# Sparse attention with a SOLU layer on one core: masks moved from GpSimd to TensorE and VectorE, products with V in a rhythm of two, one and none, later turns of k and q by DMA

## The chip, the cores and the metric

One core of a Trainium2 chip runs the kernel. The metric is device microseconds of one execution. TensorE (PE) multiplies, ScalarE (ACT) evaluates exp and ln, VectorE (DVE) and GpSimd (POOL) work on elements, SyncE (SP) issues most DMAs. Each engine works through its own instructions in order; semaphores tie them together.

## What is computed

Block-sparse attention (4 batches, 8 heads, 768 positions, 64 columns a head), then a layer on the 3072 x 512 rows that come out of it:

```python
mask = (|blk_i - blk_j| <= 1) | first or last block | sampled blocks      # blocks of 32
attn = softmax(where(mask, q @ k.T / 8, -1e9))
x    = attn @ v                       # to rows of 512: all heads of one position
h    = x @ w_in                       # 512 -> 1024
solu = h * softmax(h)
out  = (solu - mean) / sqrt(var + 1e-6) * g_ln @ w_out                    # 1024 -> 512
```

## The kernel before

The loop runs over 144 units `s` (L610), each one score block: `where(s)` gives the pass `kp` (12 passes; a pass is 256 query positions of one batch `b`), the head pair `a` (4) and `j`, a third of the keys (3). So three units make the keys of one head pair, 12 units a pass, 36 a batch. The steps of a unit:

- `score` (L321): four matmuls of 64 rows, two heads side by side in rows 0 to 63 and 64 to 127, into one of three PSUM buffers of the pool `p_s`; then one exp of 128x1024 on ScalarE into `ex` (6 buffers).
- `mask` (L335), one unit later: `ex` times a 0/1 mask kept in `mask_sb`. From unit 12 on, the middle third (`j` = 1) goes to GpSimd, the others to VectorE.
- `outs` (L343), `LAG` = 3 units later: eight matmuls with V into the single buffer `op` of the pool `p_op`. V has a column of ones, so the sum of the softmax comes with it.
- `normalise` (L359), after the products of `j` = 2: a reciprocal and a multiplication on VectorE, from `op` into `xb`. The next head pair's first product needs `op` back.

Beside this, `later` (L540) holds work by unit number, run after the unit's own steps and in the order in which it was entered. A pass gives two tiles of 128 rows of the second layer; 22 of the 24 tiles run inside the loop, one per six units, from unit M0 = 18 on. A tile `t`: `moe_x` (DMA transpose `xT`), `moe_h` in two halves of four matmuls and an exp, where `h` lies in a buffer of `p_s` from its first half until `moe_u` has multiplied it with the exp (`solu`); `moe_t` (DMA transpose `lnT`), `moe_b` (statistics, ending in `vpe`), `moe_r` (ln and exp for 1/sqrt), `moe_o` (eight matmuls in four pairs), `moe_y` (scaling on ScalarE into `ot`, and the store). The last two tiles form the tail, with transposes on TensorE.

For the batches 1 to 3, `later` also loads k, q and v of a head pair (384 KB each), casts them on GpSimd (`cast_st`, `cast_v`), and turns k and q on TensorE (`turn_kq`: six transposes into a buffer of `p_s`, and a VectorE copy). Scaling w_out with g_ln and taking its column mean away (`scale_w`, `centre_w`) are 16 GpSimd instructions in units 10 to 19. The masks are built by `make_mask` from 24-row matmuls of `vis_t` (which block sees which) with `onehot`. SP issues the loads, stores and all DMA transposes in program order.

Of the kernel before, what the change touches and what calls it, by code (L numbers as in the profile page):

```python
# [201 lines left out]
def kernel(  # L202
# [11 lines left out]
    nc = tc.nc  # L214
# [59 lines left out]
    ex_p = pool("ex", 6)  # L274
# [38 lines left out]


# [6 lines left out]
    def score(s):  # L321
        kp, b, r, a, j = where(s)
        ps = p_s.tile([TQ, 2, 512], FP32, tag="s", name=f"s{s}")
        for n in range(2):
            i = 2 * j + n
            for par in range(2):
                lo = 64 * par
                nc.tensor.matmul(ps[:, par, n * 256 : (n + 1) * 256],  # L328
                                 kTs[b][lo : lo + 64, a, i * TQ : (i + 1) * TQ],
                                 qTs[b][lo : lo + 64, a, r * 256 : (r + 1) * 256],  # L330
                                 start=(n == 0), stop=(n == 1), skip_group_check=True)
# [3 lines left out]
    def mask(s, eng):  # L335

        kp, b, r, a, j = where(s)
        eng.tensor_tensor(  # L338
            out=exs[s], in0=exs[s],
            in1=mask_sb[:, r * NJ + j : r * NJ + j + 1, :].broadcast_to([TQ, 2, 512]),  # L340
            op=ALU.mult)
# [37 lines left out]
    def moe_h(t, half):  # L379
        if half == 0:  # L380
            hs[t] = p_s.tile([128, 2, HF], FP32, tag="s", name=f"h{t}")
        for c in range(KD):
            nc.tensor.matmul(hs[t][:, half, :], xTs[t][:, c, :],  # L383
                             w_in_sb[:, c, half * HF : (half + 1) * HF],
                             start=(c == 0), stop=(c == KD - 1))
        if half:
            es_of[t] = mo.tile([128, d_ff], BF16, tag="e", name=f"e{t}")
            nc.scalar.activation(out=es_of[t], in_=hs[t].rearrange("p a b -> p (a b)"),  # L388
                                 func=ACT.Exp, scale=1.0, accum_out=esum_all[:, t : t + 1])
# [38 lines left out]
    def moe_y(t):  # L428
        ot = mo.tile([128, d_model], FP32, tag="ot", name=f"ot{t}")
        nc.scalar.activation(out=ot, in_=o_ps.pop(t), func=ACT.Copy, scale=rstds.pop(t))  # L430
# [10 lines left out]
    def scale_w(c):  # L441
        nc.gpsimd.tensor_scalar(out=w_out_sb[:, c, :], in0=w_out_f[:, c, :],  # L442
# [9 lines left out]
    def centre_w(c):  # L452
        nc.gpsimd.tensor_sub(out=w_out_sb[:, c, :], in0=w_out_sb[:, c, :], in1=mean_sb)  # L453
# [17 lines left out]
    onehot = setup.tile([NB, NT, TQ], BF16, name="onehot")  # L471
    nc.vector.memset(onehot, 1.0)
# [10 lines left out]
    for base, cm, sgn in ((0, -BLK, 1), (BLK - 1, BLK, -1)):  # L483
        nc.gpsimd.affine_select(out=onehot, in_=onehot, compare_op=ALU.is_ge, fill=0.0,
# [13 lines left out]
    cast_st(0, 0, 0, nc.vector.tensor_copy)  # L498
    cast_st(1, 0, 0, nc.vector.tensor_copy)
    turn_kq(0, 0, 0, nc.scalar.copy)  # L500
    turn_kq(1, 0, 0, nc.scalar.copy)
# [10 lines left out]
    mask_sb = setup.tile([TQ, PPB * NJ, 512], BF16, name="mask_sb")  # L512

    def make_mask(n, copy):
        m = p_s.tile([TQ, 2, 512], FP32, tag="s", name=f"m{n}")
        hi = min(2 * n + 2, PPB * NJ)
        for u in range(2 * n, hi):
            r, j = u // NJ, u % NJ
            for i in range(2):
                nc.tensor.matmul(m[:, u % 2, i * 256 : (i + 1) * 256], vis_k[:, 2 * j + i, :],  # L520
                                 onehot[:, r * QW : (r + 1) * QW, :],
                                 start=(i == 0), stop=(i == 1), skip_group_check=True)
        copy(out=mask_sb[:, 2 * n : hi, :], in_=m[:, 0 : hi - 2 * n, :])

    make_mask(0, nc.vector.tensor_copy)
# [4 lines left out]
    cast_v(0, 0, nc.gpsimd.tensor_copy)  # L530
    for a in range(1, NPR):
        for which in range(2):
            cast_st(which, 0, a, nc.gpsimd.tensor_copy)
        cast_v(0, a, nc.gpsimd.tensor_copy)
# [13 lines left out]
    for n in range(1, (PPB * NJ + 1) // 2):  # L548
        at((0, 4, 6, 8)[n - 1], make_mask, n, nc.vector.tensor_copy)
    for c in range(KF):  # L550
        at(10 + c // 2, scale_w, c)
        at(16 + c // 2, centre_w, c)
    at(15, mean_of_w)
    for b in range(1, B):
        s0 = (b - 1) * UP * PPB + 6
        at(s0 - 1, alloc_kq, b)
        for a in range(NPR):
            for which in range(3):
                at(s0 + 6 * a + which, load_raw, which, b, a, nc.sync)
            for which in range(2):  # L560
                at(s0 + 6 * a + 4 + which, cast_st, which, b, a, nc.gpsimd.tensor_copy)
                at(s0 + 6 * a + 6 + 2 * which, turn_kq, which, b, a, nc.vector.tensor_copy)
            at(s0 + 6 * a + 6, cast_v, b, a, nc.gpsimd.tensor_copy)
    n_tail = n_tiles - QW
    for t in range(n_tail):
        s0 = M0 + 6 * t
        at(s0, moe_h, t, 0)
        at(s0 + 1, moe_h, t, 1)
        at(s0 + 2, moe_u, t)
        at(s0 + 2, moe_t, t)  # L570
        at(s0 + 3, moe_b, t, 0)
        at(s0 + 4, moe_b, t, 1)
        at(s0 + 6, moe_r, t)
        for n in range(4):
            at(s0 + 8 + n, moe_o, t, 2 * n, 2 * n + 2)
        at(s0 + 11, moe_y, t)
# [22 lines left out]
    for off, fn, args in (  # L599
        (-1, turn_x, (t0, nc.scalar.copy)), (-1, turn_x, (t1, nc.vector.tensor_copy)),  # L600
        (0, moe_h, (t0, 0)), (0, moe_h, (t0, 1)), (1, moe_u, (t0,)), (1, moe_h, (t1, 0)),
        (1, moe_h, (t1, 1)), (2, turn_u, (t0,)), (2, moe_u, (t1,)), (3, moe_b, (t0, 0)),
# [5 lines left out]

    s = -1
    while s < n_units + LAG or later:  # L610
# [3 lines left out]
        if 1 <= s <= n_units:  # L614
            mask(s - 1, nc.gpsimd if (s - 1) % NJ == 1 and s > UP else nc.vector)
        if s >= LAG and s - LAG < n_units:
            u = s - LAG
            outs(u)
            if u % NJ == NJ - 1:
                kp, b, r, a, j = where(u)  # L620
# [60 lines left out]
```

## Time and profile before

| | |
|---|---|
| median of 3 runs | 306.6 us (306.16 to 308.51) |
| the profiled execution | 304.71 us, its span 303.0 us |
| busy in the span | PE 222.9 us (74%), DVE 208.8 (69%), ACT 193.6 (64%), POOL 165.6 (55%) |
| mean granted TensorE clock | 0.926 |
| DMA | 37.40 MB, mean 123 GB/s |

The span goes from the first to the last instruction; 1.7 us lie around it. No engine is busy throughout. Busy time of matmuls is modelled and overlaps, so the pace of TensorE is read from one start to the next. A wait is named after what ended it.

### The profile page before, as it was taken

To read this page: it belongs to the slowest core of one execution; us is meant where nothing else is said; L and a number is where in the kernel's file an instruction comes from. 1 tells how busy PE (TensorE), PEld (TensorE's weight loads), DVE (VectorE), ACT (ScalarE), POOL (GpSimd) and SP (SyncE) were. 2 spreads that over 40 slices of the span, in tenths; PEclk is the share of its full clock that TensorE was granted. 3 is DMA by queue.
4 is the path that set the end of the run, shared out by engine and by line. 5 is a ranking of instruction groups with operands and counts; after the bars stand their busy time and mean duration, and the time that the engine had idled before them with its cause. 6 is when DMAs were issued, how large, how long until landed. Compare 5 with 4: busy or idle time off the path is not lost.

```text
span 303.0 us, 5943 instructions
## 1 busy us (share of the span) xinstructions
PE 222.9 (74%) x2317; PEld 105.2 (35%) x2356; DVE 208.8 (69%) x402; ACT 193.6 (64%) x271; POOL 165.6 (55%) x121
## 2 busy tenths in 40 slices
PE   1789848196877687697688668678877977886862
PEld 1355414043433243343233334333323432333330
DVE  3867805748768877975966797797658468665770
ACT  2445625249677967775787687768758676973531
POOL 4946999967353856756354775746344253533000
PEclk9999967759999999997999999999979898997977
DMA  6999160506226649344326557483234032122103
GB/s 218 390 259 400 56 223 0 141 0 107 63 60 187 147 133 273 101 126 114 71 52 211 175 133 198 155 110 82 55 87 71 19 88 69 38 69 71 35 35 111
DMA packets 54405, 37.40 MB, mean 123 GB/s; under 512 B 37476, under 2 KB 49764, under 8 KB 54372
## 3 DMA queue, kind: packets, MB, share of 16 engines
q1 hardware_dynamic: 53572, 35.54, 42.0%
q0 software_dynamic: 528, 1.05, 1.8%
q8 instruction: 19, 0.31, 0.5%
q10 hardware_dynamic: 272, 0.39, 0.4%
q14 instruction: 14, 0.11, 0.1%
HBM read 23.07 MB, written 6.29 MB: 97 GB/s over the span
## 4 chain that ended last, share of the span: by engine, by line
DVE 37%; PE 32%; POOL 11%; DMA 8%; issue 7%; ACT 2%; SPq 1%; POOLq 0%; ACTq 0%
PE h L383 15%; PE op L353 9%; DVE solu L393 8%; DVE ex L338 8%; DVE stats L403 8%; PE s L328 5%; DMA w_out_f<-in_moe_w_out_dram 5%; POOL w_out_sb L442 5%; DVE vpe L411 4%; DVE xb L367 4%; DMA raw<-in_v_dram 3%; POOL w_out_sb L453 3%; DVE recip_all L365 2%; POOL ex L338 2%; PE o L425 2%
## 5 line engine op out<-in xcount | busy, mean ns | idle before, releaser
L333 ACT ACTIVATE ex<-s 128x1024 bf16<-128x1024 f32 x144 | 144.2, 1028 | 72.0 <-PE s L328 69.1
L338 POOL TENSOR_TENSOR ex<-ex,mask_sb 128x1024 bf16<-128x1024 bf16 x44 | 96.3, 2189 | 95.1 <-ACT ex L333 95.1
L353 PE MATMUL op<-v,ex 128*128 128x65 bf16 x1152 | 65.2, 203 | 47.4 <-DVE xb L367 39.9
L353 PEld LDWEIGHTS <-ex 128*128 128x128 bf16 x1152 | 47.2, 103 | 84.9 <-DVE xb L367 50.0
L338 DVE TENSOR_TENSOR ex<-ex,mask_sb 128x1024 bf16<-128x1024 bf16 x100 | 75.0, 758 | 2.0 <-ACT ex L333 2.0
L328 PE MATMUL s<-qT,kT 64*128 64x256 bf16 x576 | 61.9, 296 | 9.6 <-ACT ex L333 7.1
L365 DVE RECIPROCAL recip_all<-op 128x4 f32<-128x4 f32 x48 | 8.5, 177 | 66.8 <-PE op L353 66.8
L383 PE MATMUL h<-w_in_sb,xT 128*128 128x512 bf16 x175 | 53.0, 416 | 1.7 <-issue 0.9
L425 PE MATMUL o<-w_out_sb,lnT 128*128 128x512 bf16 x171 | 52.1, 386 | 2.4 <-ACT ot L430 1.3
L328 PEld LDWEIGHTS <-kT 64*128 64x128 bf16 x576 | 18.1, 96 | 69.2 <-issue 67.2
L403 DVE BATCH_NORM_STATS2 stats<-solu 128x6 f32<-128x512 bf16 x48 | 32.7, 685 | 0.0
L388 ACT ACTIVATE e<-h 128x1024 bf16<-128x1024 f32 x24 | 24.6, 1024 | 11.9 <-PE h L383 10.0
L393 DVE TENSOR_TENSOR solu<-h,e 128x1024 bf16<-128x1024 f32 x24 | 29.2, 1216 | 0.3 <-ACT e L388 0.3
L300 POOL CAST st<-raw 128x768 bf16<-128x768 f32 x30 | 26.4, 881 | 1.2 <-POOL st L300 0.9
L310 PE MATMUL tp<-ident,st 128*128 128x128 bf16 x192 | 19.5, 252 | 6.7 <-DVE st L300 5.8
L411 DVE TENSOR_TENSOR vpe<-vpe,mv 128x1 f32<-128x1 f32 x24 | 23.5, 981 | 0.8
L383 PEld LDWEIGHTS <-xT 128*128 128x128 bf16 x192 | 17.6, 106 | 15.2 <-issue 4.6
L367 DVE TENSOR_TENSOR xb<-op,recip_all 128x256 bf16<-128x256 f32 x48 | 20.4, 425 | 1.7
L304 POOL CAST v<-raw 128x768 bf16<-128x768 f32 x16 | 16.5, 1029 | 6.2 <-DMA raw<-in_v_dram 6.1
L430 ACT ACTIVATE ot<-o,rstd 128x512 f32<-128x512 f32 x24 | 16.6, 696 | 1.4 <-issue 1.4
L442 POOL TENSOR_SCALAR w_out_sb<-w_out_f,g_ln_sb 128x512 bf16<-128x512 f32 x8 | 13.8, 1736 | 5.7 <-DMA w_out_f<-in_moe_w_out_dram 5.7
L310 PEld LDWEIGHTS <-st 128*128 128x128 bf16 x192 | 14.0, 113 | 7.7 <-DVE st L300 5.8
(57 smaller groups left out, 101.2 us busy)
## 6 DMA issues: line engine op xcount, KB each, us to landing
raw<-in_k_dram SPq DMA_DIRECT2D x16, 384.0 KB, 4.0
raw<-in_v_dram SPq DMA_DIRECT2D x16, 384.0 KB, 5.6
out_dram<-ot SPq DMA_DIRECT2D x24, 256.0 KB, 2.1
raw<-in_q_dram SPq DMA_DIRECT2D x15, 384.0 KB, 4.7
w_out_f<-in_moe_w_out_dram SPq DMA_DIRECT2D x2, 1024.0 KB, 14.4
w_in_sb<-in_moe_w_in_dram POOLq DMA_DIRECT2D x1, 1024.0 KB, 13.1
raw<-in_q_dram ACTq DMA_DIRECT2D x1, 384.0 KB, 3.3
xT<-xb SPq DMA_TRANSPOSE x22, 2.4
```

The lines of the kernel that those rows point to most:

```text
L310: nc.tensor.matmul(tp[:, i, :], st[:, i, :], ident, is_transpose=True, start=(i == 0), stop=(i == NT - 1))
L328: nc.tensor.matmul(ps[:, par, n * 256 : (n + 1) * 256], kTs[b][lo : lo + 64, a, i * TQ : (i + 1) * TQ], qTs[b][lo : lo + 64, a, r * 256 : ...
L333: nc.scalar.activation(out=exs[s], in_=ps, func=ACT.Exp, scale=scale)
L338: eng.tensor_tensor(out=exs[s], in0=exs[s], in1=mask_sb[:, r * NJ + j : r * NJ + j + 1, :].broadcast_to([TQ, 2, 512]), op=ALU.mult)
L353: nc.tensor.matmul(op[:, par * QW + c, :], ex[:, par, lo : lo + TQ], vbuf[b % 2][:, a, par, 2 * j + n, :], start=(j == 0 and n + par + c = ...
L367: nc.vector.tensor_tensor(out=dst, in0=op[:, :, 0:D].rearrange("p (h c) d -> p h c d", h=2), in1=recip.rearrange("p (h c) o -> p h c o", h ...
L383: nc.tensor.matmul(hs[t][:, half, :], xTs[t][:, c, :], w_in_sb[:, c, half * HF : (half + 1) * HF], start=(c == 0), stop=(c == KD - 1))
L393: nc.vector.tensor_mul(out=solus[t], in0=hs.pop(t).rearrange("p a b -> p (a b)"), in1=es_of.pop(t))
L403: nc.vector.bn_stats(out=stats_of[t][:, i, :], in_=solus[t][:, i * HF : (i + 1) * HF])
L411: nc.vector.tensor_add(out=vpe, in0=vpe, in1=mv[:, 1:2])
L425: nc.tensor.matmul(o_ps[t], lnTs[t][:, f, :], w_out_sb[:, f, :], start=(f == 0), stop=(f == KF - 1))
L442: nc.gpsimd.tensor_scalar(out=w_out_sb[:, c, :], in0=w_out_f[:, c, :], scalar1=g_ln_sb[:, c : c + 1], scalar2=None, op0=ALU.mult)
```

## The change

- GpSimd only casts. `scale_w` and `centre_w` go to VectorE, six and five units later. The masks of the middle third from unit 12 on are no longer multiplied: four more matmuls of 24 rows in `score` add `hid` (0 where seen, -1e30 where not) onto the scores before the exp. `hid` and `onehot` are made once and copied by DMA to partitions 64 to 87 as well. All other masks are on VectorE, two units after the score instead of one.
- `outs` runs two units' products when `s` leaves 1 on division by 3 (units `s`-4 and `s`-3), one when it leaves 2, none when it leaves 0; `normalise` follows four units after the last score of its group.
- For the batches 1 to 3, k and q are turned by a DMA transpose on SP (`turn_dma`); a head pair's loads follow each other by five units instead of six, starting four units later.
- `moe_h` makes both halves at once; `moe_u` and what follows come one unit later; `moe_o` runs in pieces of two, three and three; `moe_y` scales on VectorE, but for the last tile; tile 21 starts three units earlier.
- At the start vis comes before the first casts, the first qT copy goes to VectorE beside ScalarE's kT copy, the first mask copy to ScalarE, and GpSimd casts v after the next k and q. `ex` has 7 buffers.

```diff
+    def turn_dma(which, b, a):
+        st = staged.pop((which, b, a)).rearrange("p i h d -> p (i h d)")
+        nc.sync.dma_start_transpose(
+            out=(kTs, qTs)[which][b][:, a, :].rearrange("p (i x) -> p i x", i=NT), in_=st)
...
     def score(s):
...
+        for n in range(2 if added else 0):
+            for par in range(2):
+                lo = 64 * par
+                nc.tensor.matmul(ps[:, par, n * 256 : (n + 1) * 256],
+                                 hid_k[lo : lo + NB, 2 * j + n, :],
+                                 onehot[lo : lo + NB, r * QW : (r + 1) * QW, :],
+                                 start=False, stop=(n == 1), skip_group_check=True)
...
+    def adds_mask(s):
+        return s >= UP and s % NJ == 1
...
     def moe_y(t):
...
-        nc.scalar.activation(out=ot, in_=o_ps.pop(t), func=ACT.Copy, scale=rstds.pop(t))
+        if t < n_tiles - 1:
+            nc.vector.tensor_scalar(out=ot, in0=o_ps.pop(t), scalar1=rstds.pop(t), scalar2=None,
+                                    op0=ALU.mult)
...
-        nc.gpsimd.tensor_scalar(out=w_out_sb[:, c, :], in0=w_out_f[:, c, :],
+        nc.vector.tensor_scalar(out=w_out_sb[:, c, :], in0=w_out_f[:, c, :],
...
+    def make_hid():
+        nc.vector.tensor_scalar(out=hid[0:NB], in0=vis_t.rearrange("a n o -> a (n o)"),
+                                scalar1=-1.0, scalar2=1e30, op0=ALU.add, op1=ALU.mult)
+        for t in (hid, onehot):
+            nc.sync.dma_start(out=t[64 : 64 + NB], in_=t[0:NB])
...
-                at(s0 + 6 * a + 4 + which, cast_st, which, b, a, nc.gpsimd.tensor_copy)
-                at(s0 + 6 * a + 6 + 2 * which, turn_kq, which, b, a, nc.vector.tensor_copy)
+                at(s0 + 5 * a + 5 + which, cast_st, which, b, a, nc.gpsimd.tensor_copy)
+                at(s0 + 5 * a + 7 + which, turn_dma, which, b, a)
...
+        s0 = M0 + 6 * t - (3 if t == n_tail - 1 else 0)
+        at(s0, moe_h, t)
+        at(s0 + 3, moe_u, t)
...
-            mask(s - 1, nc.gpsimd if (s - 1) % NJ == 1 and s > UP else nc.vector)
-        if s >= LAG and s - LAG < n_units:
-            u = s - LAG
-            outs(u)
...
+        todo = {1: (s - 4, s - 3), 2: (s - 3,), 0: ()}[s % NJ]
+        for u in todo:
+            if 0 <= u < n_units:
+                outs(u)
...
+        if 2 <= s <= n_units + 1:
+            mask(s - 2)
```

On VectorE, from a mask of tile 5 to the normalise of the next group, before (exNN is unit NN's exp, opK_A the products of pass K and head pair A):

```order
L338 TENSOR_TENSOR ex51_1530<-ex51_1530,mask_sb_196 128x1024
L403 BN_STATS stats5_1544<-solu5_1521 128x6
L406 BN_AGGR mv5_1567<-stats5_1544 128x2
L409 TENSOR_SCALAR vpe5_1569<-esum_all_62 128x1
L411 TENSOR_TENSOR vpe5_1569<-vpe5_1569,mv5_1567 128x1
L365 RECIPROCAL recip_all_61<-op4_0_1533 128x4
L367 TENSOR_TENSOR xb4_1588<-op4_0_1533,recip_all_61 128x2x2x64
L338 TENSOR_TENSOR ex53_1577<-ex53_1577,mask_sb_196 128x1024
L312 COPY kT2_1267<-tp02_1_1615 128x768
L338 TENSOR_TENSOR ex54_1603<-ex54_1603,mask_sb_196 128x1024
```

The same stretch after:

```order
L423 BN_STATS stats5_1526<-solu5_1489 128x6
L359 TENSOR_TENSOR ex51_1474<-ex51_1474,mask_sb_176 128x1024
L423 BN_STATS stats5_1526<-solu5_1489 128x6
L426 BN_AGGR mv5_1552<-stats5_1526 128x2
L429 TENSOR_SCALAR vpe5_1554<-esum_all_62 128x1
L431 TENSOR_TENSOR vpe5_1554<-vpe5_1554,mv5_1552 128x1
L386 RECIPROCAL recip_all_61<-op4_0_1504 128x4
L388 TENSOR_TENSOR xb4_1564<-op4_0_1504,recip_all_61 128x2x2x64
L451 TENSOR_SCALAR ot4_1568<-o4_1466,rstd4_1448 128x512
L359 TENSOR_TENSOR ex53_1533<-ex53_1533,mask_sb_176 128x1024
L359 TENSOR_TENSOR ex54_1562<-ex54_1562,mask_sb_176 128x1024
```

The normalise still stands behind `vpe`; `ot` has come in behind it, the mask after that is of the same unit, and the kT copy is gone.

On GpSimd in units 52 to 62, before:

```order
L338 TENSOR_TENSOR ex52_1551<-ex52_1551,mask_sb_196 128x1024
L300 CAST st12_1_1591<-raw12_1_1478 128x2x6x64
L304 CAST v0_105<-raw22_1_1516 128x12x64
L338 TENSOR_TENSOR ex55_1640<-ex55_1640,mask_sb_196 128x1024
L300 CAST st02_2_1731<-raw02_2_1624 128x2x6x64
L338 TENSOR_TENSOR ex58_1720<-ex58_1720,mask_sb_196 128x1024
```

and after, casts alone:

```order
L304 CAST v0_105<-raw22_0_1401 128x12x64
L300 CAST st02_1_1631<-raw02_1_1484 128x2x6x64
L300 CAST st12_1_1647<-raw12_1_1524 128x2x6x64
L304 CAST v0_105<-raw22_1_1546 128x12x64
L300 CAST st02_2_1771<-raw02_2_1633 128x2x6x64
L300 CAST st12_2_1795<-raw12_2_1649 128x2x6x64
```

Each mask between two casts is gone.

On SP around the transposes for tiles 6 and 7, before:

```order
L295 DMA raw02_1_1451<-in_k_dram 128x2x384
L295 DMA raw12_1_1478<-in_q_dram 128x2x384
L377 DMA_TRANSPOSE xT6_1504<-xb3_1264 128x4x128
L377 DMA_TRANSPOSE xT7_1506<-xb3_1264 128x4x128
L295 DMA raw22_1_1516<-in_v_dram 128x2x384
L398 DMA_TRANSPOSE lnT5_1523<-solu5_1521 128x8x128
L432 DMA out_0_dram<-ot4_1595 128x512
L295 DMA raw02_2_1624<-in_k_dram 128x2x384
L295 DMA raw12_2_1651<-in_q_dram 128x2x384
```

and after:

```order
L398 DMA_TRANSPOSE xT6_1478<-xb3_1245 128x4x128
L398 DMA_TRANSPOSE xT7_1480<-xb3_1245 128x4x128
L295 DMA raw02_1_1484<-in_k_dram 128x2x384
L418 DMA_TRANSPOSE lnT5_1491<-solu5_1489 128x8x128
L295 DMA raw12_1_1524<-in_q_dram 128x2x384
L316 DMA_TRANSPOSE kT2_1359<-st02_0_1482 128x6x128
L295 DMA raw22_1_1546<-in_v_dram 128x2x384
L316 DMA_TRANSPOSE qT2_1360<-st12_0_1522 128x6x128
L456 DMA out_0_dram<-ot4_1568 128x512
L295 DMA raw02_2_1633<-in_k_dram 128x2x384
L295 DMA raw12_2_1649<-in_q_dram 128x2x384
```

Between `xT7` and the store there now stand two turns, kT2 and qT2, each of which needs a cast by GpSimd, and `lnT5` stands one load further forward.

## Rows read from the trace of the kernel before

**Rows 1.** timeline, TensorE at the stage marks: start, us, engine, line, op, tiles
```profile
30.96 0.60 PE L328 MATMUL s<-qT,kT 64*128 64x256 bf16 x4
...
64.26 0.63 PE L383 MATMUL h<-w_in_sb,xT 128*128 128x512 bf16 x1
...
276.29 1.90 PE L383 MATMUL h<-w_in_sb,xT 128*128 128x512 bf16 x4
```
**Rows 2.** chain that ended last, 24 to 70 us: start, us, what, line
```profile
24.95 3.47 POOL w_out_sb L442 x2
...
55.49 3.11 POOL w_out_sb L453 x2
```
**Rows 3.** timeline, waits of products with V and vpe; bracket: idle before <- releaser
```profile
60.75 0.62 PE L353 MATMUL op<-v,ex 128*128 128x65 bf16 x8 [6.53 <-POOL ex L338]
...
245.35 0.41 PE L353 MATMUL op<-v,ex 128*128 128x65 bf16 x8 [2.08 <-DVE xb L367]
...
252.14 2.29 POOL L338 TENSOR_TENSOR ex<-ex,mask_sb 128x1024 bf16<-128x1024 bf16 x1 [1.86 <-ACT ex L333]
...
253.41 1.03 DVE L411 TENSOR_TENSOR vpe<-vpe,mv 128x1 f32<-128x1 f32 x1
...
255.05 0.62 PE L353 MATMUL op<-v,ex 128*128 128x65 bf16 x8 [2.08 <-DVE xb L367]
...
255.48 1.90 PE L383 MATMUL h<-w_in_sb,xT 128*128 128x512 bf16 x4
...
284.81 0.16 DVE L411 TENSOR_TENSOR vpe<-vpe,mv 128x1 f32<-128x1 f32 x1
```
**Rows 4.** timeline, TensorE's pieces at the low and the high level of its clock
```profile
17.43 1.05 PE L520 MATMUL m<-onehot,vis_t 24*128 24x256 bf16 x4
...
18.41 0.61 PE L328 MATMUL s<-qT,kT 64*128 64x256 bf16 x4
...
251.48 0.39 PE L328 MATMUL s<-qT,kT 64*128 64x256 bf16 x4
...
251.80 0.42 PE L353 MATMUL op<-v,ex 128*128 128x65 bf16 x8
...
252.05 0.59 PE L425 MATMUL o<-w_out_sb,lnT 128*128 128x512 bf16 x2
...
252.58 0.39 PE L328 MATMUL s<-qT,kT 64*128 64x256 bf16 x4
...
281.47 1.90 PE L383 MATMUL h<-w_in_sb,xT 128*128 128x512 bf16 x8
```
**Rows 5.** groups of instructions, 217 to 262 us: busy us, mean ns, idle before
```profile
L333 ACT ACTIVATE ex<-s 128x1024 bf16<-128x1024 f32 x26 | 25.4, 1032 | 10.0 <-PE s L328 9.9
...
L338 DVE TENSOR_TENSOR ex<-ex,mask_sb 128x1024 bf16<-128x1024 bf16 x17 | 11.2, 681 | 0.0
...
L393 DVE TENSOR_TENSOR solu<-h,e 128x1024 bf16<-128x1024 f32 x5 | 6.1, 1215 | 0.0
L403 DVE BATCH_NORM_STATS2 stats<-solu 128x6 f32<-128x512 bf16 x8 | 5.5, 686 | 0.0
...
L367 DVE TENSOR_TENSOR xb<-op,recip_all 128x256 bf16<-128x256 f32 x9 | 3.8, 424 | 0.3
...
L430 ACT ACTIVATE ot<-o,rstd 128x512 f32<-128x512 f32 x4 | 2.8, 711 | 0.0
```
**Rows 6.** groups of instructions, whole span
```profile
L338 POOL TENSOR_TENSOR ex<-ex,mask_sb 128x1024 bf16<-128x1024 bf16 x44 | 96.3, 2189 | 95.1 <-ACT ex L333 95.1
```
**Rows 7.** timeline, SP's queue, one transpose
```profile
81.80 1.24 SPq L398 DMA_TRANSPOSE lnT<-solu  x1
```
**Rows 8.** stretches: us, busy us by engine, granted clock, DMA share, GB/s
```profile
83.00:83.50 0.50, 0.50 (x7) 0.14 (x6) 0.50 (x2) 0.50 (x1) 0.00 (x0) 1.00 1.15 263
...
150.00:200.00 50.00, 38.95 (x462) 18.28 (x472) 38.53 (x73) 37.22 (x54) 28.97 (x20) 1.00 0.54 151
```
**Rows 9.** DMA issues: xcount, median us from issue to landing
```profile
xT<-xb SPq DMA_TRANSPOSE x22, 2.4
```

## What I expect and why

> **What bounds the kernel now.** I read the profile in four cuts, because one average over it would mix stages with different limits: the three marks of the timeline between the stages, then the chain that ended last in the second stage, the timeline of one clean tile in the third, and the groups of instructions with their means. Call the loop's step for one score block a unit (144 of them), and six units with one tile of the second layer a tile. The marks cut the span of 303.0 us [rows 1]: to the score of unit 12 at 30.96 (A, 31.0 us), to the first h matmul of tile 1 in unit 24 at 64.26 (B, 33.3 us), to the first h matmul of tile 21 in unit 144 at 276.29 (C, 212.0 us, that is 20 tiles of 10.60 us), and the tail (D, 26.7 us).
>
> In B the chain of waits runs on GpSimd without a break: scaling of w_out from 24.95, centring until 58.6, with masks and casts in between [rows 2], and at its end the products with V had waited 6.53 us for a GpSimd mask [rows 3]. Twelve units took 33.3 us there, 2.8 us each, against 1.77 us in C.
>
> In C take the tile whose waits stand alone [rows 3]. GpSimd's mask runs from 252.14 to 254.43. VectorE's vpe, an addition of one column, starts at 253.41 and lasts 1.03 us until GpSimd is done; with GpSimd idle the same instruction took 0.16 us (284.81). The normalise behind it on VectorE is late by that, and TensorE, which may not write the single "op" buffer before it is emptied, stands idle for 2.08 us at 255.05. The four h matmuls after the wait took 1.90 us [rows 3], as long as all eight of a whole h at 281.47 [rows 4]: the clock had fallen. So the bound of C is no engine, but a loop TensorE -> ScalarE -> GpSimd -> VectorE -> TensorE, once per tile.
>
> **Part by part.** TensorE's pieces, start to start at the high level of the clock [rows 4]: the score of a unit 0.32 us (251.48 to 251.80), its products with V 0.25, two o matmuls 0.53 to the next score; a whole h is 1.90. A tile before is 6 x 0.32 + 6 x 0.25 + 4 x 0.53 + 1.90 = 7.44, and about 0.2 for h cut in two. With the wait of 2.08 that is 9.7; from 245.35, where the previous wait ended, to 255.05 it is 9.70 [rows 3]. The method holds for before, so I use it for after.
>
> *Masks on TensorE.* 44 masks leave GpSimd (2.19 us each [rows 6]) and become four 24-row matmuls each, two per tile. No row shows 24-row matmuls in pairs of row groups. Cheap end: like the score, two pairs on rows 0 and 64: 0.32 less a switch, 0.21. Dear end: one after the other as the mask building does it, 0.98 us for four at the low clock (17.43 to 18.41) [rows 4], 0.55 with the columns at twice the rate and the same 0.12 overhead. I take 0.33, the score's price with its switch, because the operands stand at partitions 0 and 64 as the score's do: 0.66 per tile, 44 x 0.33 = 14.5 us of TensorE in all. The Trainium skill, TensorEngine Tiling (Array Packing), Key Properties, says that row tiles run independently but that changing the tiling mode drains the engine. By the first half the four matmuls cost 0.21, by the second 0.12 more, as a score of 64 rows is followed by tiles of 32; priced by the building row instead they would add 44 x 0.22 = 9.7 us to the sum.
>
> *Products with V later, in a rhythm of 2, 1, 0.* Costs nothing on TensorE. The normalise now has, between the last product of a group and the first of the next, the whole of a unit without products and a further score, at least 0.32 + 0.75 + 0.65 us of TensorE work. Lay out a tile from its first score: score 0.0; h to 2.2; masked score and two units of products to 3.35; score, products, two o to 4.46; score and three o to 5.5; the next (masked) score must wait for the exp before last, since h holds one of three score buffers: exps of 1.03 us [rows 5] behind h's put it at 5.8, a stall of 0.3; products to 7.0; score, products, three o to 8.3. VectorE in the same frame: normalise 4.1 to 4.7, solu to 5.8, mask, stats, mask, stats to 8.2, vpe to 8.7, normalise to 9.3, ot to 9.9, two masks to 11.1, and it waits for the next normalise at 12.4. What TensorE needs from it comes 1.7 us early or more. ot costs VectorE 0.71 as on ScalarE, at the dear end; if that cover is gone, the normalise is late by what lacks, as before.
>
> *Sums per tile.* TensorE 7.44 + 0.66 + stall 0.3 = 8.4, less 0.1 for fewer switches. VectorE 4 x 0.68 + 1.22 + 2 x 0.69 + 2 x 0.42 + 0.71 for ot, and 0.9 for six small ones (vpe at 0.16 [rows 3]): some 7.8 by means [rows 5]. ScalarE 6 x 1.03, and about one and a half exps more for h and rstd, some 7.8, without the 0.71 of ot. TensorE sets the tile: 8.3 clean. Before, the mean tile was 10.60 where the clean one was 9.70, 0.9 more (turns with their copies, casts, clock). Turns and copies leave the engines; GpSimd's casts can still hold masks on VectorE as its mask held vpe, and VectorE has 1.3 us to spare in the frame. I add 0.55: 8.85. Bounds: 8.3 and 9.8 (masks at 0.55, 0.5 of new waits, all the old excess).
>
> *Turns by DMA.* 24 of the 32 turns leave TensorE and VectorE for SP. An issue of lnT (256 KB) holds SP 1.24 us [rows 7]; a turn (192 KB) the same or three quarters of it. At 1.24 it is 30 us more on a queue that also issues xT and lnT. In twelve units of a loading stretch SP then has four old transposes, two stores, seven loads and five turns, some 15 us of 17.7. Followed through the order, xT of tile 6 is issued right after its normalise (4.7 in the frame) and lands 2.4 us later [rows 9], 1.2 us before h wants it (8.3); lnT of tile 7, behind a turn and a load, lands about when o wants it. While lnT's 256 KB move, at 263 GB/s, the DMA engines show a share of 1.15 [rows 8], so it is 1.15 us of all of them; a turn is then 0.86 us, eight per batch 7 us in some 35. With the shorter tiles that lifts the share of 0.54 [rows 8] to about 0.85. Hidden, at little margin.
>
> *w_out on VectorE.* Neither stands on VectorE before. A mask of 1024 columns takes 0.68 [rows 5], so 512 columns 0.34 at the cheap end, twice that at the dear one: I take 0.4 for the eight scalings and 0.34 for the eight subtractions, 6 us, between units 16 and 24 where VectorE has 9 us of its own (six masks, three normalises, one solu with its stats). GpSimd's chain is gone. I take units 12 to 16 at 1.15 us (an exp and a little), then 13.4 us for VectorE's work: B = 18 (15 to 24).
>
> *Start and end.* The first qT copy runs beside kT's instead of behind it, GpSimd casts k and q before v: A = 28.5 (27 to 31; the low clock of TensorE stays). In the tail tile 21 is three units earlier and its 2.4 us wait goes, one normalise later: D = 25 (23.5 to 27).
>
> The sum is 28.5 + 18 + 177 + 25 = 248.5 of span, against 303.0; with the 1.7 us that lie around the span of this execution (304.71) 250.2. The runs' median is 306.6, 0.6% above that execution, so 252.
>
> **Rivals.** *TensorE or VectorE dearer:* masks at 0.55, drains, masks of VectorE behind casts: C at 9.3 to 9.8, 262 to 272. For: no row prices the 24-row pairs. Against: VectorE's slack.
>
> *Transposes late:* SP in order makes xT or lnT wait behind a turn that waits for a GpSimd cast; h or o then stands 2 to 4 us in the 12 tiles of the three loading stretches: 24 to 48 us, 277 to 300. For: SP is 85% full there. Against: the casts are due two units ahead of the turns, and kT and qT are needed only a pass later.
>
> *The gain is not there:* VectorE, which gets GpSimd's work on w_out and ScalarE's ot, becomes the chain in GpSimd's place, in B and in C, at the old pace: 306.6. It would take 2.8 us a unit in B and 10.6 a tile in C, where its work by rows is 15 us for nine units and 7.8 a tile.
>
> *Slower:* the clock. At the low one of its two levels (1.2 GHz) a score is busy for 0.61 us against 0.39 (18.41, 251.48) [rows 4], so 4.1 us of scores, masks and products become 6.4, and the 4.0 of h and o near 7.6: a tile of 14.2, 5.4 more. If TensorE were at that level for half of C (54 of 20 x 5.4 us), the kernel would be no faster, beyond that slower. For: a wait of 2 us cost 0.9 us on four h matmuls [rows 3], and new waits might be many. Against: from 150 to 200 the granted clock was 1.00 with such a wait in the tiles [rows 8], and after, TensorE has fewer.
>
> **How the numbers follow.** Chances: the forecast 0.62 (its own range 243 to 262), dearer engines 0.16, still cheaper than 243 0.06, late transposes 0.08, gain not there 0.03, slower by the clock 0.05. The range 239 to 277 leaves out 2 in 10. A measurement tells about 1% here, 3 us. Faster by over 1%: 0.92; within 1%: 0.03; slower: 0.05.
>
> **What would show it.** The h matmuls of tile 1 near 46 us and of tile 21 near 220; tiles of 8.3 to 9; vpe at 0.2 us or so where GpSimd is idle; no wait of products with V for the normalise over 0.5 us; the mask's matmuls adding 0.3 us to a score; GpSimd busy under 50 us. Wrong if TensorE waits for xT or lnT, if VectorE is busy without gaps in C, if the mask's matmuls take 0.5 us or more, or if the granted clock is low in C.

## The result and the profile after

The changed kernel takes 262.7 us (261.3 to 263.0) against 306.4 us before: a ratio of 0.855 (95% interval 0.850 to 0.861). The forecast was 252.0 with a range of 239 to 277: the side and the range hold, the point is 10.7 us short. The profiled execution has a span of 260.8 us, where the sum forecast 248.5. Times below are medians of executions at the undisturbed clock; the runs with the masks back on GpSimd and with the rhythm undone have only one of these, so no ratio, and from the traces of the masks back on GpSimd and of the mask's matmuls made twice, which are of disturbed executions, only durations on VectorE and GpSimd or a stretch at a granted clock of 1.00 are read.

The page of after: busy time of each engine, and the DMA engines' busy share in 40 slices of the span (tenths).

```profile
PE 217.8 (83%) x2347; PEld 105.5 (40%) x2384; DVE 196.7 (75%) x417; ACT 177.2 (68%) x248; POOL 44.4 (17%) x61
...
DMA  6999539899422999999532779999144731413012
```

TensorE is now busy for 83% (74% before), GpSimd for 44.4 us (165.6 before). The digits of the DMA line stand at or near 9 at the start and in three stretches of the loop, one for each batch that is loaded there.

The marks of [rows 1] in the timeline of after: unit 12's score, then the first h matmuls of tiles 1 and 20 (start, us, engine, line, op, tiles).

```profile
29.34 0.64 PE L334 MATMUL s<-qT,kT 64*128 64x256 bf16 x8
...
47.16 3.17 PE L404 MATMUL h<-w_in_sb,xT 128*128 128x512 bf16 x7 [0.33 <-issue]
...
224.10 1.90 PE L404 MATMUL h<-w_in_sb,xT 128*128 128x512 bf16 x7
```

Tile 21 is three units earlier than before, so the stages are compared up to h of tile 20 (266.41 before):

| stage | before | forecast | after |
|---|---|---|---|
| A, to unit 12 | 31.0 | 28.5 | 29.3 |
| B, to h of tile 1 | 33.3 | 18 | 17.8 |
| 19 tiles, to h of tile 20 | 202.1 (10.64 each) | 168.2 (8.85 each) | 176.9 (9.31 each) |
| from there to the end | 36.6 | 33.9 | 36.7 |

(The last forecast is 8.85 + 25.) Of 12.3 us missing in the span, 8.7 are in the loop and 2.8 in its last tiles and the tail.

A clean tile of after, answering to [rows 3, 4]: the scores with mask, the products, vpe and the normalise.

```profile
83.11 0.42 PE L342 MATMUL s<-onehot,hid 24*128 24x256 bf16 x4
...
83.47 0.66 PE L374 MATMUL op<-v,ex 128*128 128x65 bf16 x16
...
85.91 0.16 DVE L431 TENSOR_TENSOR vpe<-vpe,mv 128x1 f32<-128x1 f32 x1
...
86.19 0.42 DVE L388 TENSOR_TENSOR xb<-op,recip_all 128x256 bf16<-128x256 f32 x1
```

vpe is at 0.16 us where it was 1.03, no product waits for the normalise in this tile, and the mask's four matmuls add 0.36 us (83.11 to 83.47). Five tiles without loads, from 183.07 to 224.10, take 8.21 us each; the frame of the forecast said 8.3.

What TensorE waits for instead is late transposes. Waits of after over the whole span (engine, line, releaser: us in total, times, longest).

```profile
PE h L404 <- DMA xT<-xb: 9.4, 4, 4.3
PE o L445 <- DMA lnT<-solu: 5.2, 3, 2.1
```

The longest of them in the timeline of after, with the normalise that xT needs and SP's queue ahead of it.

```profile
108.23 0.42 DVE L388 TENSOR_TENSOR xb<-op,recip_all 128x256 bf16<-128x256 f32 x1
...
108.86 0.43 SPq L295 DMA_DIRECT2D raw<-in_k_dram  x1
109.34 0.55 SPq L295 DMA_DIRECT2D raw<-in_q_dram  x1
109.99 3.49 SPq L398 DMA_TRANSPOSE xT<-xb  x2
...
116.82 2.31 PE L404 MATMUL h<-w_in_sb,xT 128*128 128x512 bf16 x5 [4.26 <-DMA xT<-xb]
119.35 1.06 PE L404 MATMUL h<-w_in_sb,xT 128*128 128x512 bf16 x2 [0.22 <-issue]
```

Two transposes hold SP for 3.49 us instead of 2.5, xT lands 6.8 us after its issue ([rows 9]: 2.4), and after the wait the clock is at the low of its two levels (granted 0.50 from 116.80 to 120.40): the eight h matmuls run from 116.82 to 120.35, 3.53 us instead of 1.83. Of the lateness some 1.3 us are the queue (the normalise ends at 108.65, a store and two loads are issued before xT at 109.99), and 4.4 the slower landing.

DMA issues of after (count, median us from issue to landing), and three stretches (us, busy us by engine, granted clock, DMA share, GB/s): two while a batch is loaded, one with no loads.

```profile
lnT<-solu SPq DMA_TRANSPOSE x22, 4.1
kT<-st SPq DMA_TRANSPOSE x12, 4.3
...
95.00:120.00 25.00, 18.35 (x192) 8.30 (x194) 16.31 (x34) 14.39 (x21) 7.11 (x9) 0.90 1.16 243
...
150.00:175.00 25.00, 20.06 (x223) 9.28 (x224) 19.49 (x42) 17.12 (x23) 6.51 (x8) 0.96 1.07 238
...
180.00:230.00 50.00, 49.43 (x570) 23.38 (x580) 42.49 (x92) 43.21 (x62) 0.00 (x0) 1.00 0.38 83
```

The share where a batch is loaded is 1.16 and 1.07; the forecast said 0.85, from the 0.54 of [rows 8]. (From 95 to 120 us of before it was 0.68.) The share adds up the times of the packets, so that a value above 1 says that packets of one engine overlap in time.

### The profile page after: what moved, and what is told of

It is laid out like the page before. It is cut to its first block, busy times and chain, and to the rows that moved or that the text cites. A ratio compares the mean times of both kernels' runs of the same rounds, so it can differ in the third digit from the quotient of the medians.

```text
span 260.8 us, 5955 instructions
## 1 busy us (share of the span) xinstructions
PE 217.8 (83%) x2347; PEld 105.5 (40%) x2384; DVE 196.7 (75%) x417; ACT 177.2 (68%) x248; POOL 44.4 (17%) x61
## 4 chain that ended last, share of the span: by engine, by line
PE 61%; DVE 16%; DMA 14%; issue 2%; ACT 2%; SPq 1%; POOL 1%; POOLq 0%
PE h L404 14%; PE s L334 13%; PE o L445 13%; PE op L374 12%; DMA lnT<-solu 7%; DMA xT<-xb 6%; DVE ex L359 5%; PE s L342 4%; DVE solu L413 2%; DVE stats L423 2%; PE tp L310 2%; DMA raw<-in_q_dram 1%; DVE w_out_sb L477 1%; PE m L541 1%; DVE xb L388 1%
## 5 line engine op out<-in xcount | busy, mean ns | idle before, releaser
L359 DVE TENSOR_TENSOR ex<-ex,mask_sb 128x1024 bf16<-128x1024 bf16 x100 | 70.9, 728 | 2.3 <-ACT ex L347 2.2
L404 PE MATMUL h<-w_in_sb,xT 128*128 128x512 bf16 x176 | 48.8, 409 | 11.3 <-DMA xT<-xb 9.4
L374 PE MATMUL op<-v,ex 128*128 128x65 bf16 x1152 | 53.7, 197 | 5.2 <-DVE ex L359 4.5
L374 PEld LDWEIGHTS <-ex 128*128 128x128 bf16 x1152 | 41.7, 99 | 26.1 <-issue 12.8
L408 ACT ACTIVATE e<-h 128x1024 bf16<-128x1024 f32 x24 | 24.6, 1024 | 34.6 <-PE h L404 34.6
L445 PEld LDWEIGHTS <-lnT 128*128 128x128 bf16 x192 | 14.7, 100 | 19.4 <-issue 6.8
L342 PE MATMUL s<-onehot,hid 24*128 24x256 bf16 x176 | 18.9, 293 | 0.0
L451 DVE TENSOR_SCALAR ot<-o,rstd 128x512 f32<-128x512 f32 x23 | 17.1, 744 | 0.0
L310 PE MATMUL tp<-ident,st 128*128 128x128 bf16 x48 | 6.3, 306 | 6.3 <-DVE st L300 6.3
L342 PEld LDWEIGHTS <-hid 24*128 24x128 bf16 x176 | 7.5, 131 | 9.7 <-issue 9.7
L436 ACT ACTIVATE lnv<-vpe 128x1 f32<-128x1 f32 x24 | 4.9, 202 | 6.2 <-DVE vpe L431 6.2
```

Source lines behind the costliest of these rows:

```text
L342: nc.tensor.matmul(ps[:, par, n * 256 : (n + 1) * 256], hid_k[lo : lo + NB, 2 * j + n, :], onehot[lo : lo + NB, r * QW : (r + 1) * QW, :], ...
L359: nc.vector.tensor_tensor(out=exs[s], in0=exs[s], in1=mask_sb[:, m : m + 1, :].broadcast_to([TQ, 2, 512]), op=ALU.mult)
L374: nc.tensor.matmul(op[:, par * QW + c, :], ex[:, par, lo : lo + TQ], vbuf[b % 2][:, a, par, 2 * j + n, :], start=(j == 0 and n + par + c = ...
L404: nc.tensor.matmul(hs[t][:, half, :], xTs[t][:, c, :], w_in_sb[:, c, half * HF : (half + 1) * HF], start=(c == 0), stop=(c == KD - 1))
L445: nc.tensor.matmul(o_ps[t], lnTs[t][:, f, :], w_out_sb[:, f, :], start=(f == 0), stop=(f == KF - 1))
```

## The experiments

Two questions: what made the transposes late, and whether the gain has the causes that the forecast named. For the first, "theory 1" stands for this: the turns fill the DMA engines, so that transposes issued among them land late. Its rival is the order in SP's queue.

### The turns left out

```diff
     def alloc_kq(b):
+        if b:
+            kTs[b], qTs[b] = kTs[0], qTs[0]
+            return
...
-                at(s0 + 5 * a + 7 + which, turn_dma, which, b, a)
```

> The changed kernel without the 24 turns: batches 1 to 3 take k and q of batch 0 (loads and casts stay, so the output is another one). This prices the turns whole. Theory 1: no wait for xT or lnT in the loop beyond the first, all tiles near 8.3 us, 244 to 250 us. If the waits come from the loads alone: still 256 or more.

251.7 us, ratio to before 0.818 (0.813 to 0.823). The turns cost 11.0 us, as much as the forecast's miss of 10.7 (which has other parts too: the 2.8 us of the last tiles and tail aren't theirs). It stays above the 244 to 250 that theory 1 gave: o still waits for lnT 5.1 us, so lnT is late without a turn, at a DMA share of 0.83 from 95 to 120 us. The share of queue q1 tells what a turn takes of the DMA engines (packets, MB, share of 16 engines' span); after first, then this run.

```profile
q1 hardware_dynamic: 72844, 40.33, 65.3%
```

```profile
q1 hardware_dynamic: 53644, 35.61, 52.7%
```

0.653 x 260.8 less 0.527 x 251.3 is 37.9 us of packet time for 24 turns, 1.58 us each. The forecast had 0.86. The figure moves with the traffic: the same subtraction from the other runs below with the same transfers in the same queue gives 1.2 to 1.7.

### The turns back on TensorE

```diff
-                at(s0 + 5 * a + 7 + which, turn_dma, which, b, a)
+                at(s0 + 5 * a + 7 + which, turn_kq, which, b, a, nc.vector.tensor_copy)
```

> The changed kernel with one part undone: the 24 turns of k and q of batches 1 to 3 go back to TensorE, with a copy by VectorE. In the changed kernel TensorE waited 9.4 us for xT and 5.2 us for lnT. Theory 1 (the turns fill the DMA engines, so that transposes issued among them land 5 to 7 us after their issue): these waits go, xT lands again in 2.4 us and lnT in under 3; TensorE pays some 0.5 us a turn for six transposes (12 us) and perhaps a wait for a score buffer; net 255 to 264 us against 262.7. Rival (the waits come from the loads and the transposes themselves, with shorter tiles): the waits stay, and with the turns' price the time is 270 to 278.

255.7 us, 0.832 (0.828 to 0.836), as theory 1 had it. h waits for no transpose in the loop, and lnT costs one wait; the second fence shows one turn:

```profile
PE o L445 <- DMA lnT<-solu: 0.7, 1, 0.7
```

```profile
94.69 0.50 PE L310 MATMUL tp<-ident,st 128*128 128x128 bf16 x6
```

The DMA share from 95 to 120 us is 1.03 here, higher than the 0.83 of the run without turns, and yet o waits less (0.7 us for 5.1). So the share alone doesn't tell how long TensorE waits.

This part of the change, as placed, made the kernel 7.0 us slower: 24 turns on TensorE, busy for 0.50 us each, cost less than the waits that the same turns by DMA brought.

### The same DMAs, wider apart

```diff
-                at(s0 + 5 * a + which, load_raw, which, b, a, nc.sync)
+                at(s0 + 7 * a + which, load_raw, which, b, a, nc.sync)
...
```

(Casts and turns likewise: 7 * a for 5 * a.)

> The changed kernel with a head pair's loads (and casts and turns) seven units after the last one's instead of five; the same bytes and the same DMAs in the same order within a head pair. Theory 1 (the DMA engines are full in the loading stretches): a stretch is 29 units long instead of 23, the DMA share falls by a quarter, and most of the 14.6 us of waits for xT and lnT go: 248 to 254 us. Rival (SP's queue in order, its head waiting for casts): each head pair has the same queue, the casts stand as near to the turns as before, and the waits stay, or are fewer only by what falls between the head pairs: 257 to 263.

255.9 us, 0.836 (0.831 to 0.840), 6.8 us faster than the changed kernel. Between the two forecasts, nearer the rival's: of the waits, 7.3 us for xT and 3.5 for lnT are left. Density matters, but a wider spacing doesn't remove the late transposes.

### No turn at the head of SP's queue waits for a cast

```diff
-    stage = pool("stage", 3)
+    stage = pool("stage", 6)
...
-                at(s0 + 5 * a + 7 + which, turn_dma, which, b, a)
+                at(s0 + 5 * a + 9 + which, turn_dma, which, b, a)
```

> The changed kernel with six stage buffers instead of three and each turn two units later behind its cast: GpSimd's casts no longer wait for a turn to empty a buffer (19.8 us in the changed kernel), and no turn at the head of SP's queue waits for a cast. Rival (SP in order, the step that the prediction named): the late xT and lnT come from this, so their 14.6 us of waits go for the most part: 249 to 255 us. Theory 1 (DMA engines full): the same bytes in the same stretch, the waits stay within a third: 258 to 265.

257.4 us, 0.839 (0.836 to 0.843), 5.3 us faster. The casts no longer wait for a turn, but this leaves 10.8 us of waits (4.9 for xT, 5.9 for lnT) of 14.6. By the waits theory 1 holds; the time lies just under its band, so some of the gain may be the order on SP. The run moves the turns by two units as well, so it doesn't say which of its two edits did it.

### The loads in a queue of their own

```diff
-                at(s0 + 5 * a + which, load_raw, which, b, a, nc.sync)
+                at(s0 + 5 * a + which, load_raw, which, b, a, nc.scalar)
```

> The changed kernel with the 36 loads of batches 1 to 3 issued from ScalarE's queue instead of SP's; the same bytes at the same places of the program. Rival A (the transposes wait behind the loads and turns that SP issued before them, one queue in order): with the loads in a queue of their own xT lands in under 4 us and lnT in under 4, most of the 14.6 us of waits go: 248 to 255 us, if ScalarE's issues cost it nothing. Theory 1 (the 16 DMA engines are full, whichever queue): the waits stay within a third: 258 to 265. If issues hold ScalarE (0.44 us each on its queue), 36 of them cost up to 16 us: up to 275.

264.0 us, 0.860 (0.853 to 0.868): no gain. Waits and issues to landing of this run:

```profile
PE h L404 <- DMA xT<-xb: 11.9, 5, 3.8
```

```profile
raw<-in_k_dram ACTq DMA_DIRECT2D x12, 384.0 KB, 3.8
...
xT<-xb SPq DMA_TRANSPOSE x22, 4.1
lnT<-solu SPq DMA_TRANSPOSE x22, 4.6
```

Rival A falls. In a queue of their own the loads of k land in 3.8 us (median; in the changed kernel the median over all, the start's among them, is 5.5), and xT, with no load ahead of it in its queue, lands later than before, 4.1 us for 2.3 (medians). So the place behind the loads isn't what makes the transposes late. The turns still stand in SP's queue here, so this run doesn't clear them.

### More lead for the transposes

```diff
-        s0 = M0 + 6 * t - (3 if t == n_tail - 1 else 0)
+        s0 = M0 + 6 * t - (3 if t == n_tail - 1 else 0) + (3 if t < 17 else 0)
...
+        elif t < 17 - 2:
+            for off, lo, hi in ((11, 0, 2), (12, 2, 5), (14, 5, KF)):
+                at(s0 + off, moe_o, t, lo, hi)
+            at(s0 + 15, moe_y, t)
```

(Tiles 15 and 16 run o in two pieces, to come back to the old places.)

> The changed kernel, all DMAs as they are, with more lead for the transposes: h, solu and what follows of tiles 0 to 16 come three units later, so that xT has three more units before h wants it, and the o matmuls of tiles 0 to 14 another three, so that lnT has eight units instead of five. Theory 1a (in the loading stretches the transposes are slow, at 5 to 7 us, but the DMA engines keep up over a stretch): the waits of 14.6 us and the low clock behind them go: 246 to 252 us. Rival (the engines fall behind over a whole stretch, or the casts and the stage buffers back up): the waits only move; 257 to 263.

253.4 us, 0.824 (0.817 to 0.832), 9.2 us faster. No wait for a transpose is left in the loop. It missed the 246 to 252 because tiles of that stretch took 8.83 us, also those without loads: o and h had come into the same unit, and one unit on the score waits for an exp (the next run tests this).

```profile
101.04 0.39 PE L334 MATMUL s<-qT,kT 64*128 64x256 bf16 x4 [0.44 <-ACT ex L347]
...
113.59 1.89 PE L404 MATMUL h<-w_in_sb,xT 128*128 128x512 bf16 x8
...
122.42 1.89 PE L404 MATMUL h<-w_in_sb,xT 128*128 128x512 bf16 x8
```

### More lead, and o away from h

```diff
-        elif t < 17 - 2:
-            for off, lo, hi in ((11, 0, 2), (12, 2, 5), (14, 5, KF)):
+        elif t < 18 - 3:
+            for off, lo, hi in ((14, 0, 2), (15, 2, 5), (17, 5, KF)):
```

(Here the shift of h goes to tile 17, and tiles 15 to 17 run o three units apart.)

> The run with more lead, but the o matmuls of tiles 0 to 14 six units later against h instead of three, so that o falls again in other units than h (in the run with three, both stood in one unit, the next score waited 0.44 us for an exp, and all its tiles took 8.83 us, those clean of DMA too). Theory (the transposes only lack lead, and the place of o within the tile cost the 0.62 us): no wait for xT or lnT, tiles of 8.21 us also in the loading stretches, 16 times 0.62 us less than 253.4, and one to three us for three tiles' o closer together at the end: 244 to 248 us. Rival (at 8.21 us a tile the DMA engines, at a share of 0.80 with tiles of 8.83, do not keep up, and the waits come back): 250 to 257.

246.4 us, 0.802 (0.798 to 0.807): the fastest version, 16 us under the changed kernel. Timeline of this run at the place of the long wait above, and the same stretch as above.

```profile
111.03 1.90 PE L404 MATMUL h<-w_in_sb,xT 128*128 128x512 bf16 x7 [1.16 <-DMA xT<-xb]
...
119.24 1.90 PE L404 MATMUL h<-w_in_sb,xT 128*128 128x512 bf16 x7
```

```profile
95.00:120.00 25.00, 23.63 (x282) 11.20 (x285) 20.04 (x44) 20.84 (x30) 7.96 (x8) 1.00 1.15 250
```

One wait of 1.16 us is left, tiles take 8.21 us under load too, and the DMA share is that of the changed kernel (1.15 for 1.16). The engines keep up over a stretch, while single transposes among loads are still slow (the slowest xT lands after 5.1 us, lnT after 5.3). What the changed kernel lacked was lead.

### The mask's matmuls made twice

```diff
-        for n in range(2 if added else 0):
+        for n in (0, 1, 0, 1) if added else ():
```

> The changed kernel with the mask's four matmuls made twice in each of the 44 units (minus 2e30 instead of minus 1e30, the exp is the same 0). Prices the matmuls and tells what bounds a tile. Theory (TensorE sets the clean tile at 8.2 us, and the four cost 0.33 us): 44 times 0.33 is 14.5 us, a clean tile 8.87; where TensorE stood waiting for transposes a few us are hidden: 272 to 277 us. Rival (VectorE, 7.8 us a tile by means, is as near the bound, or the matmuls cost 0.21): 266 to 270. Dear end (0.55 each): 285.

266.4 us (266.2 to 267.7), 0.873 (0.866 to 0.880): 3.5 to 5.0 us more, as the rival had it. The clean tiles of this run, granted clock 1.00:

```profile
193.12 1.90 PE L404 MATMUL h<-w_in_sb,xT 128*128 128x512 bf16 x7
195.28 0.64 PE L342 MATMUL s<-onehot,hid 24*128 24x256 bf16 x8
...
201.76 1.90 PE L404 MATMUL h<-w_in_sb,xT 128*128 128x512 bf16 x7
```

8.64 us against 8.21, so 0.22 us for four more matmuls where TensorE sets the pace; 44 of them would be 9.7. That the waits for transposes and the stages bound by others hide the rest is likely, but not shown. The added matmuls lengthen a clean tile by their whole price, so TensorE is its bound. The first four cost 0.36, 0.14 more than the four behind them; that this is the change from 64 rows to 24 is a reading of the difference, and no run isolates it.

### The masks back on GpSimd, in the changed kernel

```diff
     def adds_mask(s):
-        return s >= UP and s % NJ == 1
+        return False
...
+        eng = nc.gpsimd if s > UP and s % NJ == 1 else nc.vector
-        nc.vector.tensor_tensor(
+        eng.tensor_tensor(
```

> The changed kernel with one part undone: the middle thirds' 44 masks go back to GpSimd (2.19 us each), and the four 24-row matmuls of each leave TensorE. Theory (the rhythm of two, one, none leaves the normalise 1.7 us of room): vpe is held by GpSimd again, by about 1 us, but the normalise takes that from its room; TensorE has 14.5 us less to do, VectorE becomes the bound at 8 to 8.8 us a tile: 255 to 266 us against 262.7. Rival (the loop through GpSimd is what the masks cost, whatever the rhythm): waits of products with V for the normalise or for the GpSimd mask of 1 to 2 us a tile come back, tiles of 9.2 to 9.7: 278 to 290.

288.8 us, 26 us more than the changed kernel: the theory's 255 to 266 falls, and the time lies in the rival's 278 to 290. Groups of this run (busy us, mean ns):

```profile
L360 DVE TENSOR_TENSOR ex<-ex,mask_sb 128x1024 bf16<-128x1024 bf16 x100 | 109.7, 1116 | 0.8 <-ACT ex L347 0.7
L360 POOL TENSOR_TENSOR ex<-ex,mask_sb 128x1024 bf16<-128x1024 bf16 x44 | 99.0, 2249 | 102.0 <-ACT ex L347 47.4 <-ACT lnv L437 37.7 <-issue 10.0
...
L432 DVE TENSOR_TENSOR vpe<-vpe,mv 128x1 f32<-128x1 f32 x24 | 15.5, 647 | 0.8
```

and the same group of after:

```profile
L359 DVE TENSOR_TENSOR ex<-ex,mask_sb 128x1024 bf16<-128x1024 bf16 x100 | 70.9, 728 | 2.3 <-ACT ex L347 2.2
```

The room that I had given to vpe alone was taken by VectorE's own masks: 1.12 us instead of 0.73, 38.8 us in all, and 11 for vpe. One of them in this run's timeline:

```profile
156.32 2.12 POOL L360 TENSOR_TENSOR ex<-ex,mask_sb 128x1024 bf16<-128x1024 bf16 x1 [1.53 <-issue]
...
156.94 2.04 DVE L360 TENSOR_TENSOR ex<-ex,mask_sb 128x1024 bf16<-128x1024 bf16 x1
```

VectorE's mask starts behind GpSimd's and ends at 158.98, 0.54 us after it. Masks, vpe and the work on w_out have longer means in this run; solu, which reads PSUM, and the statistics stayed at 1.22 and 0.68.

### The masks on TensorE alone, in the kernel before

```diff
     def mask(s, eng):
+        if s > UP and s % NJ == 1:
+            return
```

(with `hid`, its copies and the four matmuls as in the change)

> The kernel before with one part of the change alone: the 44 masks of the middle third as four 24-row matmuls on TensorE, all else as before (products of one unit a step, turns on TensorE, w_out on GpSimd). Theory (the loop through GpSimd and vpe sets C): vpe is no longer held, the wait of products with V of 2.08 us a tile falls to 1 us or less; TensorE adds 0.66 a tile: 9.2 to 9.7 us a tile against 10.6, and some 4 us in B: 280 to 291 us. If the masks alone bring all of C: 265 to 272. Rival (VectorE's own work is what holds the normalise): 298 or more.

282.0 us, 0.919 (0.912 to 0.927), as expected: 24.6 us faster than before. vpe has a mean of 0.17 us; the wait of [rows 3], 2.08 us a tile, is 0.85:

```profile
226.26 0.42 PE L367 MATMUL op<-v,ex 128*128 128x65 bf16 x8 [0.85 <-DVE xb L381]
...
235.44 0.41 PE L367 MATMUL op<-v,ex 128*128 128x65 bf16 x8 [0.85 <-DVE xb L381]
```

A clean tile is 9.18 us where it was 9.70: 0.72 dearer by two masks at 0.36, 1.23 cheaper by the wait.

### w_out on VectorE alone, in the kernel before

```diff
-        nc.gpsimd.tensor_scalar(out=w_out_sb[:, c, :], in0=w_out_f[:, c, :],
+        nc.vector.tensor_scalar(out=w_out_sb[:, c, :], in0=w_out_f[:, c, :],
...
-        at(10 + c // 2, scale_w, c)
-        at(16 + c // 2, centre_w, c)
+        at(16 + c // 2, scale_w, c)
+        at(21 + c // 2, centre_w, c)
```

> The kernel before with one part of the change alone: scaling and centring of w_out on VectorE, in the changed kernel's units. Theory (in stage B the chain of GpSimd sets the end): tile 1's h comes 11 to 15 us earlier and C keeps its pace of 10.6 us a tile: 291 to 296 us against 306. Rival (GpSimd's masks and casts hold B by themselves, or VectorE becomes the chain): 301 to 306.

301.9 us, 0.986 (0.977 to 0.995): 4.6 us, not 11 to 15. h of tile 1 comes at 61.96, 2.3 us earlier, and the wait of 6.53 us in [rows 3] has another name:

```profile
60.91 0.62 PE L353 MATMUL op<-v,ex 128*128 128x65 bf16 x8 [6.05 <-DVE xb L367]
```

This is the rival's forecast, 301 to 306. VectorE took GpSimd's place in the chain: with masks still on GpSimd, a scaling took 0.82 us and a centring 0.74, against 0.48 and 0.53 in the changed kernel.

### The rhythm undone

```diff
-        todo = {1: (s - 4, s - 3), 2: (s - 3,), 0: ()}[s % NJ]
+        todo = (s - 3,)
...
-        u = s - (3 if last else 4)
+        u = s - 3
```

> The changed kernel with one part undone: products with V of one unit a step again, three units after the score, and the normalise right behind them, so that the next group's first products follow after one score and an h or two o. Theory: the normalise must run within that, behind a mask, stats or solu on VectorE; waits of some 1 us for it come back once or twice a tile: 275 to 290 us. Rival (the rhythm is worth nothing once vpe is no longer held): 261 to 266.

282.6 us, 20 us more than the changed kernel: the size expected, by another wait. A tile takes 9.29 us (199.89 to 209.18), and the products wait for masks, not for the normalise:

```profile
199.89 0.42 PE L374 MATMUL op<-v,ex 128*128 128x65 bf16 x8 [0.53 <-DVE ex L359]
...
204.00 0.42 PE L374 MATMUL op<-v,ex 128*128 128x65 bf16 x8 [0.36 <-DVE ex L359]
...
209.18 0.42 PE L374 MATMUL op<-v,ex 128*128 128x65 bf16 x8 [0.53 <-DVE ex L359]
```

The run keeps the masks two units behind the score, which the rhythm was made with, and so doesn't separate the two. What the rhythm would cost with masks one unit behind wasn't tried.

## Why the prediction was right, and where it was short

**The bound.** Right. The loop through GpSimd's mask and vpe set stage C: the masks alone bring 24.6 of the 43.7 us, and put back on GpSimd they cost at least 26. The price of holding was read too narrowly: I saw it on vpe only, since VectorE's masks took 0.68 in the clean stretch of before [rows 5]. The Trainium skill, SBUF — State Buffer, SBUF: two separate sides, has the two engines share a port pair that one instruction locks for its whole length; the traces agree (vpe 1.03 and 0.16, masks 1.12 and 0.73, and the held mask above).

**Masks on TensorE.** 0.33 forecast, 0.36 measured. The Trainium skill, TensorEngine Tiling (Array Packing), Key Properties, as weighed there, fits in both halves: 0.22 for four without a new change of mode, and 0.14 more with one, as far as the difference of two rows can say.

**Stage B.** 18 forecast, 17.8 measured, but the step was right for a joint reason. "GpSimd's chain is gone" holds only because the masks left GpSimd too; the move of w_out by itself brought the h of tile 1 forward by 2.3 us, the whole change by 17.1 (64.26 to 47.16). The number owes something to luck: the work on w_out took VectorE 7.4 us, not 6, and VectorE was busy for 11.4 of the 14.2 us from unit 16 on, so its work alone doesn't make up the 13.4 of the forecast. Units 12 to 16 took some 3.6 us, not 4.6.

**The tile.** 8.3 forecast, 8.21 measured without loads; the rhythm hides the normalise (no wait for it over 0.5 us in C), ot on VectorE (0.74) is hidden. The stall of 0.3 for an exp didn't come (in the five tiles without loads TensorE has no wait in the list of waits): 7.44 and two masks at 0.36 are 8.16.

**Turns by DMA: the step that failed.** "Hidden, at little margin" costed them at nothing; they cost 11.0 us, and TensorE waited for xT and lnT, which the prediction had named as a sign that it was wrong. Three things were mis-sized. A turn takes 1.2 to 1.7 us of the DMA engines' packet time (1.58 above; 1.29 by the run with later turns, 0.639 x 255.6 less 132.4, over 24), not the 0.86 that came from the rate of a lone lnT [rows 8]. The 0.85 also left out that the loads follow each other by five units instead of six: 0.54 x 10.60 / 8.85 and 7 us in 35 give 0.85, and with 6 / 5 on the first term 0.98. Measured were 1.07 to 1.16. And I took a median over all transposes [rows 9], 2.4 us, for those among loads, where xT took up to 6.8 and lnT up to 6.0. The median of xT is still 2.3 in after. The trace of before had the warning; landing of its xT, then of its lnT:

```profile
DMA to landing us min/median/max: 2.3/2.4/4.2
```

```profile
DMA to landing us min/median/max: 2.7/2.8/5.9
```

The margin of 1.2 us that the forecast gave xT was less than this spread. The rival "transposes late" named the waits, with another cause and two to four times the price. SP's order is a part of it, at most half by the run with later turns (5.3 of 11.0), and a queue of their own for the loads gained nothing. Whether the engines' share or the latency of each packet makes the transposes slow, the runs don't separate; that they keep up when given lead, they show.

**The addition of 0.55 a tile** was meant for casts that hold masks. 9.31 less 8.21, 1.1 a tile, was measured: 20.9 us over 19 tiles, of which 13.1 are waits for DMA and some 3.3 the h matmuls at the low clock behind two of them; the other 4.5 aren't traced here.

**The end.** 2.8 us from h of tile 20 on did not come off. There VectorE's masks let the products wait 1.83 us at 236.42, and the granted clock is 0.91 from 230 on. That was not tested.

**The clock.** The rival against did not come: the granted clock is 1.00 in the stretch without loads, and falls behind the waits of 4.26 and 3.09 us (0.50 and 0.57 in the stretches after them), as behind that of 2.08 in [rows 3], but not behind one of 2.06 for lnT at 99.82 (1.00 from 99 to 103).

## What to carry to other kernels

A transfer is not hidden because its bytes fit: read the longest landing among the traffic that it will meet, not the median, and give what waits for it that much lead. Here moving the consumers by three to nine units was worth 16 us, once o stood away from h. Work moved from TensorE to the DMA engines can cost more than it saves: as placed, the turns cost 7.0 us more by DMA than on TensorE. With lead, the kernel with turns by DMA is 9 us under the one with turns on TensorE, but the latter was not tried with the same lead. And where two engines hold each other, moving one piece of work gives little while another still holds: w_out alone gave 4.6 us with the masks left on GpSimd. The masks alone gave 24.6, and the whole change 43.7; what w_out gives once the masks are gone was not measured by itself.

## What the runs showed of the hardware

A turn of 192 KB takes 1.2 to 1.7 us of the DMA engines' packet time by the subtractions above, about as long as a load of 384 KB. In the run with loads in a queue of their own:

```profile
q10 hardware_dynamic: 10064, 14.55, 19.9%
```

37 loads, 0.199 x 262.1 us, 1.41 us each. The Trainium skill, Advanced Engine Details and Errata, X-Bar Transpose (TRN2), calls transposing DMAs as fast as regular ones; the runs differ: by these rows a byte that is turned takes about twice as long, at packets of some 250 bytes (4.72 MB in 19200 packets) and in mixed traffic.

A mask of 1024 columns on VectorE takes 0.68 us alone. Beside 44 masks on GpSimd its mean was 1.12 us, with a median of 0.69 and a longest of 2.89: some stand, most are untouched. VectorE's instructions that read PSUM kept their time (solu 1.22, ot 0.74).
